# Narrower 120-row pieces, uneven over the rows, in a grouped 1x1 convolution

## The chip, the core and the metric

The kernel runs on one core of one Trainium2 chip. The metric is device time in microseconds (us). Most executions of one kernel lie within 0.5 us of each other; about one in five is longer (by 0.7 to 2.1 us). Ratios are computed as the mean time of one kernel's fast runs over that of the other's fast runs in the same rounds on the same chip, so they are not quite the ratios of the medians that are quoted.

## The reference

```
# x: (1, 512, 512, 192) bf16, w: (1, 1, 4, 48, 48) bf16
xg  = x.reshape(1, 512, 512, 4, 48)
out = einsum('bhwgc,gcd->bhwgd', xg, w[0, 0]).reshape(1, 512, 512, 192)
```

Every pixel (192 values, 384 bytes) is read once, multiplied by four 48x48 matrices and written once: 100.7 MB in and 100.7 MB out.

## The kernel before

Pixels are dealt to 128 rows (partitions). A "column" is one pixel on each row. SyncE issues the loads into a ring of three slots of 80 columns, TensorE transposes four columns at a time, VectorE copies the transposes out of PSUM, TensorE multiplies, ScalarE casts the product into an output ring and issues the stores.

What matters here is the plan of the transfers. Nearly all of them are `FULL`: 128 rows. Twice in the run, after 6 and after 11 further slots, a slot of 80 columns is filled in two parts: a **120-row piece** that leaves out rows 16 to 19 and 48 to 51, and a full piece for the rest of the slot. The blocks of a 120-row piece are listed as (queue, first row, rows, outer size, columns fewer):

```python
FULL = (("sync", 0, 128, 128, 0),)

PARTIAL = (
    ("sync", 0, 16, 4, 0), ("sync", 32, 16, 4, 0),
    ("pool", 52, 44, 11, 0), ("pool", 20, 12, 3, 0), ("pool", 96, 32, 8, 0),
)
UNEVEN = (("sync", 0, 16, 4, 16), *PARTIAL[1:])
FRONT = ((6, ((48, PARTIAL), (32, FULL))), (11, ((48, UNEVEN), (32, FULL))))

FILL_ROWS = 5
FILL_BEFORE = (2, 3)

# plan_fields: what the gaps leave out comes back as more columns at the end
    cols = npix - sum((n - b[4]) * b[2] for n, blocks in parts for b in blocks)

# transfers: the DRAM side of a block is seen as (outer, rows / outer, pixels)
            px = ap[pix:pix + rows * cols, :]
            ...
                view = px.rearrange("(c a i) n -> a c (i n)", a=outer, c=rows // outer)
            yield n, view, tile[r0:r0 + rows, at * C:(at + (c1 - c0 if f.full else cols)) * C]

# GpSimd: a tiny filler transfer of 5 rows ahead of some of its blocks
                    for n, dram, sbuf in transfers(xf, ring, p, ("pool",)):
                        if n in FILL_BEFORE:
                            filler()
                        gp.dma_start(sbuf, dram).then_inc(ld_sem[ld_key[p.i, n]], 16)
```

The rows in the gap keep stale values; their products are computed and never stored.

Of the kernel before, what the change touches and what calls it, by code (L numbers as in the profile page):

```python
# [38 lines left out]
FULL = (("sync", 0, 128, 128, 0),)  # L39

PARTIAL = (
    ("sync", 0, 16, 4, 0), ("sync", 32, 16, 4, 0),
    ("pool", 52, 44, 11, 0), ("pool", 20, 12, 3, 0), ("pool", 96, 32, 8, 0),
)
UNEVEN = (("sync", 0, 16, 4, 16), *PARTIAL[1:])
FRONT = ((6, ((48, PARTIAL), (32, FULL))), (11, ((48, UNEVEN), (32, FULL))))

FILL_ROWS = 5
FILL_BEFORE = (2, 3)


class Field:
# [31 lines left out]
def plan_fields(npix):  # L84

    parts, head = [], sum(HEAD)
    for slots, special in FRONT:
        parts += [(head + BIG * slots, FULL), *special]
# [91 lines left out]
def bass_standalone__grouped__vision_kernel(nc, x, w, out):  # L180
# [23 lines left out]
    def transfers(ap, tile, part, queues):  # L204
        f, c0, c1, at = part.field, part.c0, part.c1, part.at
        for n, (queue, r0, rows, outer, pix, cols) in enumerate(f.blocks):
            if queue not in queues:
                continue
            px = ap[pix:pix + rows * cols, :]
            if f.full:  # L210
                view = px.rearrange("(p i) n -> p (i n)", p=rows)[:, c0 * C:c1 * C]
            else:
                assert (c0, c1) == (0, f.cols)
                view = px.rearrange("(c a i) n -> a c (i n)", a=outer, c=rows // outer)
            yield n, view, tile[r0:r0 + rows, at * C:(at + (c1 - c0 if f.full else cols)) * C]
# [12 lines left out]
    with ExitStack() as es:  # L228
# [36 lines left out]
        def freed(p):  # L265

            return max(0, -(-(4 * p.g1 - RCOLS) // 8))

        @block.gpsimd
        def _(gp):  # L270
            gp.memset(esel[:], 1.0).then_inc(p0_sem, 1)  # L271
            gp.memset(ident[:], 1.0).then_inc(p1_sem, 1)  # L272
            gp.wait_ge(p0_sem, 1)
            gp.affine_select(out=esel[:], in_=esel[:], pattern=[[-1, ECOLS]],  # L274
                             compare_op=AluOpType.is_equal, fill=0.0, base=ESHIFT,
                             channel_multiplier=1).then_inc(e_sem, 1)
            gp.wait_ge(p1_sem, 1)
            gp.affine_select(out=ident[:], in_=ident[:], pattern=[[-1, 128]],  # L278
                             compare_op=AluOpType.is_equal, fill=0.0, base=0,
                             channel_multiplier=1).then_inc(id_sem, 1)  # L280
            used = []

            def filler():
                k = len(used)
                src = xf[0:2 * FILL_ROWS, 0:4].rearrange("(t p) n -> p t n", t=2)
                dst = fill[:, 8 * k:8 * k + 8].rearrange("p (t n) -> p t n", t=2)
                gp.dma_start(dst, src).then_inc(fill_sem[k], 16)  # L287
                used.append(k)

            for nth, u in enumerate(mixed):  # L290
                part = [p for p in u.pieces if not p.full]
                for p in part:
                    gp.wait_ge(t_done, freed(p))
                    for n, dram, sbuf in transfers(xf, ring, p, ("pool",)):
                        if n in FILL_BEFORE:
                            filler()
                        gp.dma_start(sbuf, dram).then_inc(ld_sem[ld_key[p.i, n]], 16)  # L297
                for p in u.pieces:
                    for n in range(len(p.blocks)):
                        gp.wait_ge(ld_sem[ld_key[p.i, n]], 16)  # L300
                gp.sem_inc(ld_sem[unit_keys[u][0]], 16)  # L301
                gp.wait_ge(go_sem, nth + 1)
                for i, s in enumerate(stores):
                    if any(s.field is p.field for p in part):
                        for n, dram, sbuf in transfers(of, oring, s, ("pool",)):
                            if n in FILL_BEFORE:
                                filler()
                            gp.dma_start(dram, sbuf).then_inc(st_sem[i][n], 16)  # L308
            for k in used:
                gp.wait_ge(fill_sem[k], 16)  # L310
# [174 lines left out]
```

## Time and profile before

| | before |
|---|---|
| median of the runs | 476.39 us |
| span of the profiled run | 474.6 us |
| bytes moved, mean rate | 201.54 MB, 425 GB/s |
| TensorE / ScalarE / VectorE busy | 90% / 82% / 52% |
| DMA busy (three queues, 16 engines) | 99.3% |

How to read it: the busy shares of the compute engines are high, but none is full, while all sixteen DMA engines are full from the second slice to the last but one. The prediction below shows these lines. What a page does not give is which of the sixteen engines is busy with what; that was worked out from the packet records of the trace, as the prediction describes.

### The profile page before, as it was taken

The numbers are of one execution on the slowest core, as the hardware profiler recorded it, in microseconds if no ns is written. First come the engines' busy times: TensorE is split into PE (matmuls) and PEld (weight loads), VectorE is DVE, ScalarE is ACT, GpSimd is POOL, SyncE is SP. The second block draws the span as 40 slices with busy tenths as digits, with TensorE's granted clock in tenths as the row PEclk, the third lists the DMA queues.
The fourth block names the chain that finished last, engine by engine and source line by source line (L and its number), as shares of the span: only waits on it lengthen the run. The fifth ranks groups of instructions, "written<-read, shape, count | busy, mean of one in ns | idle before, by whom it ended". The sixth has DMA issues, their size and how long they took to land.

```text
span 474.6 us, 13600 instructions
## 1 busy us (share of the span) xinstructions
PE 428.2 (90%) x6178; PEld 386.2 (81%) x6178; DVE 246.8 (52%) x258; ACT 388.4 (82%) x515; POOL 12.5 (3%) x28
## 2 busy tenths in 40 slices
PE   5999999999598999999999997989698997999990
PEld 4888898888487888888888986888597896988880
DVE  2655555555344555565555554545445553555550
ACT  2999998888567998889899986888678995998982
POOL 1000000200002000000000000100002000000000
PEclk9999999999889999999999999999979998999997
DMA  8999999999999999999999999999999999999997
GB/s 330 437 396 429 432 425 432 423 429 436 433 439 426 424 436 424 436 441 429 433 429 437 420 433 431 439 417 437 432 437 418 435 433 423 437 423 436 434 419 325
DMA packets 10528, 201.54 MB, mean 425 GB/s; under 512 B 2096, under 2 KB 2096, under 8 KB 2736
## 3 DMA queue, kind: packets, MB, share of 16 engines
q1 hardware_dynamic: 4320, 97.44, 48.1%
q10 hardware_dynamic: 4976, 97.42, 47.9%
q0 software_dynamic: 1216, 6.49, 3.3%
q8 instruction: 7, 0.11, 0.1%
q14 instruction: 9, 0.07, 0.0%
HBM read 100.68 MB, written 100.66 MB: 424 GB/s over the span
## 4 chain that ended last, share of the span: by engine, by line
PE 63%; DMA 20%; ACT 10%; another core or an unknown queue 2%; issue 1%; ACTq 1%; SPq 0%; POOLq 0%
PE o_ps L371 37%; PE xT_ps L351 27%; DMA out_dram<-oring 11%; ACT oring L450 10%; DMA ring<-in_x_dram 10%; ACTq L431 1%; SPq L321 0%; SPq L314 0%; ACTq L424 0%; POOLq L301 0%; POOLq L300 0%; ACTq L433 0%
## 5 line engine op out<-in xcount | busy, mean ns | idle before, releaser
L450 ACT CAST oring<-o_ps 128x768 bf16<-128x768 f32 x514 | 387.1, 801 | 76.6 <-PE o_ps L371 55.1
L413 DVE COPY xT_sb<-xT_ps 128x1536 bf16<-128x1536 bf16 x257 | 246.2, 958 | 212.4 <-PE xT_ps L351 212.4
L371 PE MATMUL o_ps<-wt,xT_sb 128*128 128x144 bf16 (+1 forms) x3084 | 288.4, 236 | 23.7 <-ACT oring L450 18.4
L371 PEld LDWEIGHTS o_ps<-wt,xT_sb 128*128 128x128 bf16 x3084 | 211.3, 99 | 62.2 <-ACT oring L450 52.4
L351 PE MATMUL xT_ps<-ident,ring 128*128 128x128 bf16 x3084 | 220.4, 222 | 9.9 <-POOLq L301 6.0
L351 PEld LDWEIGHTS xT_ps<-ident,ring 128*128 128x128 bf16 x3084 | 188.1, 99 | 13.2 <-POOLq L301 6.2
L287 POOL DMA_DIRECT2D fill<-in_x_dram x8 | 4.6, 573 | 349.4 <-PE xT_ps L351 227.0
L297 POOL DMA_DIRECT2D ring<-in_x_dram x6 | 3.3, 559 | 0.0
L308 POOL DMA_DIRECT2D out_dram<-oring x6 | 3.3, 555 | 0.0
L333 PE MATMUL o_ps<-w_sb,esel 48*128 48x48 bf16 x10 | 0.6, 211 | 2.8 <-DMA w_sb<-in_w_dram 2.8
L333 PEld LDWEIGHTS o_ps<-w_sb,esel 48*128 48x128 bf16 x10 | 0.5, 111 | 2.8 <-issue 2.8
L406 DVE CAST wt<-o_ps 128x480 bf16<-128x480 f32 x1 | 0.7, 657 | 3.4 <-PE o_ps L333 3.4
L450 ACT ACT_TABLE_LOAD x1 | 1.3, 1283 | 0.8 <-PEq L470 0.8
L274 POOL TENSOR_SCALAR_AFFINE_SELECT esel<-esel 48x272 bf16<-48x272 bf16 x1 | 0.4, 402 | 0.0
L271 POOL MEMSET esel<- 48x272 bf16 x1 | 0.3, 318 | 0.3 <-POOLq L470 0.3
L278 POOL TENSOR_SCALAR_AFFINE_SELECT ident<-ident 128x128 bf16<-128x128 bf16 x1 | 0.3, 282 | 0.0
L272 POOL MEMSET ident<- 128x128 bf16 x1 | 0.2, 198 | 0.0
L470 POOL MEMSET const-float32-0.0<- 128x1 f32 x1 | 0.1, 98 | 0.3 <-issue 0.3
L470 POOL MEMSET const-bfloat16-1.0<- 128x1 bf16 x1 | 0.1, 101 | 0.0
L470 POOL MEMSET const-uint8-127<- 128x1 uint8 x1 | 0.1, 101 | 0.0
L470 POOL MEMSET const-float32-1.0<- 128x1 f32 x1 | 0.1, 98 | 0.0
## 6 DMA issues: line engine op xcount, KB each, us to landing
ring<-in_x_dram SPq DMA_DIRECT2D x22, 3840.0 KB, 28.3
out_dram<-oring ACTq DMA_DIRECT2D x16, 3456.0 KB, 41.0
out_dram<-oring ACTq DMA_DIRECT2D x5, 3648.0 KB, 38.2
out_dram<-oring ACTq DMA_DIRECT2D x3, 1536.0 KB, 33.4
out_dram<-oring ACTq DMA_DIRECT2D x2, 2112.0 KB, 19.8
ring<-in_x_dram SPq DMA_DIRECT2D x2, 1536.0 KB, 38.1
out_dram<-oring ACTq DMA_DIRECT2D x1, 3072.0 KB, 36.5
out_dram<-oring ACTq DMA_DIRECT2D x1, 2688.0 KB, 51.0
```

What stands on the lines that cost most here:

```text
L274: gp.affine_select(out=esel[:], in_=esel[:], pattern=[[-1, ECOLS]], compare_op=AluOpType.is_equal, fill=0.0, base=ESHIFT, channel_multipli ...
L287: gp.dma_start(dst, src).then_inc(fill_sem[k], 16)
L297: gp.dma_start(sbuf, dram).then_inc(ld_sem[ld_key[p.i, n]], 16)
L308: gp.dma_start(dram, sbuf).then_inc(st_sem[i][n], 16)
L333: last = pe.matmul(o_ps[:, NOB - 1, col:col + CG], lhsT=esel[:, s0:s0 + 128], rhs=w_sb[:, g, :], start=True, stop=True, skip_group_check=True)
L351: last = pe.transpose(xT_ps[:, g % NXP, j * 128:(j + 1) * 128], xg[:, j * 128:(j + 1) * 128], ident[:])
L371: last = pe.matmul(o_ps[:, v % NOB, c0_:c1_], lhsT=xs[:, j * 128:(j + 1) * 128], rhs=wt[:, WOFF[tc]:WOFF[tc] + (c1_ - c0_)], start=(tc == ...
L406: dve.tensor_copy(wt[:], o_ps[:, NOB - 1, 0:WCOLS]).then_inc(wc_sem, 1)
L413: dve.tensor_copy(xT_sb[pair % NXS][:, 0:n * 2 * UC].rearrange("p (g c) -> p g c", g=n), xT_ps[:, b0:b0 + n, 0:2 * UC]).then_inc(e_done[pa ...
L431: act.dma_start(dram, sbuf).then_inc(st_sem[i][n], 16)
L450: act.copy(out_columns(g).rearrange("p (u c) -> p u c", u=2), o_ps[:, v % NOB:v % NOB + 2, 0:UC]).then_inc(fa_done[g % (2 * NTOK)] if g < ...
L470: nc = _bacc.Bacc("TRN2", target_bir_lowering=False, num_devices=1)
```

## The change

The change makes both 120-row pieces narrower (48 to 40 columns, the full pieces behind them grow from 32 to 40), so that the DMA engine that moves rows 16 to 19 and 48 to 51, called engine 4 here (the names are told with the prediction), is relieved less. In the second piece it shortens rows 96 to 127 by 4 columns and cuts the block of rows 0 to 15 into four quarters with different widths. As blocks are now numbered differently, the fillers are tied to the first row of a block instead of its number.

```diff
-UNEVEN = (("sync", 0, 16, 4, 16), *PARTIAL[1:])
-FRONT = ((6, ((48, PARTIAL), (32, FULL))), (11, ((48, UNEVEN), (32, FULL))))
+UNEVEN = (
+    ("sync", 0, 4, 1, 12), ("sync", 4, 4, 1, 16), ("sync", 8, 4, 1, 20), ("sync", 12, 4, 1, 16),
+    *PARTIAL[1:4], ("pool", 96, 32, 8, 4),
+)
+FRONT = ((6, ((40, PARTIAL), (40, FULL))), (11, ((40, UNEVEN), (40, FULL))))
 
 FILL_ROWS = 5
-FILL_BEFORE = (2, 3)
+FILL_BEFORE = (52, 20)
...
-                        if n in FILL_BEFORE:
+                        if p.field.blocks[n][1] in FILL_BEFORE:
```

More of the change, by code (lines that the diff above doesn't have):

```diff
@@ L305, in _ @@
                         for n, dram, sbuf in transfers(of, oring, s, ("pool",)):
-                            if n in FILL_BEFORE:
+                            if s.field.blocks[n][1] in FILL_BEFORE:
                                 filler()
```

## The prediction

The packet records carry no engine number, so the engine numbers in this document are names for groups of rows. The groups can be read from the traces. Linked by their gaps alone (a packet starts 3 to 4 ns before the end of the one before it), the records of the changed kernel from 303 to 337 us, where its second 120-row piece is loaded, form sixteen chains; one early link is ambiguous:

- Four carry one packet of each quarter (10,752, 9,216, 7,680 and 9,216 bytes) and four of the block of rows 32 to 47 (15,360 bytes): "engines 0 to 3", or "of rows 0 to 15".
- One carries no packet of the piece, so that its eight rows are the eight left out. It holds 30 of the 32 lengthened packets, with 1.36 us of lengthening in all: the slow engine, "engine 4".
- Three carry eight packets of the two blocks of rows 20 to 31 and 52 to 95: "engines 5 to 7".
- Eight carry four packets of these blocks and four of rows 96 to 127: "engines 8 to 15", or "of rows 64 to 127".

Each of the sixteen carries eight packets of the full piece that follows. Which number is which inside a group, and which of rows 52 to 95 are whose, is not shown. In the kernel before, four chains have four packets of each of the two 16-row blocks (12,288 and 18,432 bytes, from 306 to 322 us), eleven have packets of the GpSimd blocks, and one, the lengthened one, has none of the piece.

The even split of a quarter over four engines (the 96 pixels per engine below) was an estimate: the trace showed it for 16-row blocks, not for blocks of 4 rows. That the store queue hides the three stores more rests on this: the store issued at 342.8 us took 52.2 us to land, so stores were waiting around 345 us.

> **What bounds the kernel now.** I read the slice table first, then the queues, the groups, the waits, the last of the timeline, and last the single DMA packet records of the trace.
>
> ```profile
> PE   5999999999598999999999997989698997999990
> DMA  8999999999999999999999999999999999999997
> GB/s 330 437 396 429 432 425 432 423 429 436 433 439 426 424 436 424 436 441 429 433 429 437 420 433 431 439 417 437 432 437 418 435 433 423 437 423 436 434 419 325
> ...
> q1 hardware_dynamic: 4320, 97.44, 48.1%
> q10 hardware_dynamic: 4976, 97.42, 47.9%
> q0 software_dynamic: 1216, 6.49, 3.3%
> ```
>
> The DMA row is full in every slice but the first and the last. The three queues add up to 48.1 + 47.9 + 3.3 = 99.3% of sixteen engines' span (q1 loads, q10 stores, q0 what GpSimd issues). No compute engine is so full:
>
> ```profile
> PE 428.2 (90%) x6178; PEld 386.2 (81%) x6178; DVE 246.8 (52%) x258; ACT 388.4 (82%) x515; POOL 12.5 (3%) x28
> ...
> L450 ACT CAST oring<-o_ps 128x768 bf16<-128x768 f32 x514 | 387.1, 801 | 76.6 <-PE o_ps L371 55.1
> L371 PE MATMUL o_ps<-wt,xT_sb 128*128 128x144 bf16 (+1 forms) x3084 | 288.4, 236 | 23.7 <-ACT oring L450 18.4
> L351 PE MATMUL xT_ps<-ident,ring 128*128 128x128 bf16 x3084 | 220.4, 222 | 9.9 <-POOLq L301 6.0
> ```
>
> PE's only long wait is 6.0 us for the first mixed piece, and the DMA row stays at 9 through it. The chain of waits gives PE 63%[...]; I do not take that for the bound. The timeline of the end settles it:
>
> ```profile
> 464.62 0.34 ACTq L431 DMA_DIRECT2D out_dram<-oring  x1
> 465.00 0.80 ACT L450 CAST oring<-o_ps 128x768 bf16<-128x768 f32 x1 [0.21 <-issue]
> 465.83 0.34 ACTq L431 DMA_DIRECT2D out_dram<-oring  x1
> ```
>
> The last store is issued at 466.2 us of a 474.6 us span, so the final 8 us are a backlog of stores. The kernel ends when the last of sixteen DMA engines has emptied its queue. The question is only **which engine is last, and by how much**.
>
> The packet records have a start, a duration, a size and a queue, but no engine number. A 30,720-byte packet takes 1,138 ns (27.0 bytes per ns) nearly every time, and the next packet on the same engine starts 3 to 4 ns before the end of its predecessor. So I chained records by these gaps and by each engine's known list of packets. Two things came out. (1) Counting open packets, from 20 us to 465 us there is no stretch of 150 ns in which fewer than sixteen are open: no engine ever starves. (2) One chain holds nearly every lengthened packet (the 27,648-byte packets take 1,030 to 1,150 ns there, 1,025 elsewhere), about 19.5 us of excess in all, some 5% of its work. That chain holds none of the packets of the 120-row pieces. This is the slow engine, and **relieving it is what the 120-row pieces are for**.
>
> The finish of each chain before the end of the run: the slow engine 5.8 us; the four chains that fit the list of the engines of rows 0 to 15: 3.9, 3.2, 0.3 and 0.2 us; the others from 2.9 to 0.0 us. The very last one fits rows 64 to 127 and rows 20 to 31 about equally well.
>
> [...]
>
> **The change part by part.** All in pixels per engine; a pixel is 384 bytes in and 384 out, 768 / 27.0 = 28.4 ns of its engine.
>
> *Compute:* nothing. Columns in all stay 2,056: the missing pixels were 8 x 48 + 8 x 48 + 16 x 16 = 1,024, and are now 8 x 40 + 8 x 40 + 4 x (12 + 16 + 20 + 16) + 32 x 4 = 1,024. The instruction lists show the same 514 evictions, and the same PE work.
>
> *Engine 4:* its gap shrinks from 96 to 80 columns of 8 rows: +128 pixels, 98 KB, 128 x 28.4 ns = +3.64 us; with 5% of slowness +3.8. Its finish moves from 5.8 us before the end to about 2.0 us before it. It was early, so this costs nothing.
>
> *Engines 8 to 15:* 4 columns on 4 rows each: -16 pixels, -0.45 us.
>
> *Engines 5 to 7:* unchanged. Their latest is about 0.9 us before the end (or 0.0, if the last chain is one of them).
>
> *Engines 0 to 3:* the second piece's load of 16 rows x 32 columns becomes four of 4 rows x 28, 24, 20 and 24 columns. [...] 28 + 24 + 20 + 24 = 96 pixels per engine, where there were 4 x 32 = 128. The first piece gives 4 x 8 = 32 fewer as well, and the two full pieces behind them, 32 columns and now 40, give 32 more each: the total of each engine is **unchanged**. Two of these engines end 0.2 and 0.3 us before the end.
>
> *Issues:* three more loads and three more stores. An issue on ACT took 0.34 us, so ACT loses 1.0 us around 345 us; it is 82% busy, and the store queue is never empty, so this is hidden.
>
> *Sum:* if the last engine is one of 8 to 15, it moves 0.45 us earlier, and the next, an engine of rows 0 to 15 at 0.2 us, sets the end: -0.2 us. If it is one of 5 to 7: 0.0. I take -0.1: 476.39 - 0.1 = **476.3 us**.
>
> **The rivals.**
>
> *The slow engine becomes the last.* It would have to gain over 5.8 us; it gains 3.8. Against this too: its late position in the middle. Its loads land +2.8 us behind those of a normal engine at their worst (near 295 us), and the first relief shrinks by 1.8 us, so +4.6 us. Loads take 28.3 us from issue to landing, and PE never waited for a plain load over 1.6 us, so at most a short PE stall. If the whole 3.8 us counted: 480.
>
> *The quarter transfers fall on one engine* [...]. Engine 0 would then carry 4 x 96 = 384 pixels instead of 96: +288, +8.2 us, an end at up to 484.5. [...]
>
> *Each quarter goes to its own engine,* as 12, 16, 20, 16 suggests was meant: +16, 0, -16, 0 pixels, so 0.45 us either way on two of the four engines. Depending on which two are late: 475.9 to 476.6.
>
> *A gain beyond this* has no place: all finishes at their mean would be about 2 us earlier (474.4), and the change moves under 0.5 us off any engine that is late.
>
> **Range and chances.** Runs before spread by 0.4 us (476.16 to 476.57). The named effects reach from -0.5 to about +1.5 us; I give the range 475.5 to 477.6. Over 2% either way is 9.5 us: faster is out of reach by the sum above (0.01); slower needs the one-engine rival and something more (0.02); within 2%: 0.97.
>
> **What would show it.** Right: the same PE, ACT and DVE busy times; the DMA row full up to the last slice; slow engine's chain ending about 2 us before the end instead of 5.8; q1 and q10 packet counts up only by the few packets of the split. Wrong: one chain of engines 0 to 3 ending several us after the others (one-engine rival); the slow chain last; PE waiting longer than 6.0 us for a mixed piece, or a slice of the DMA row below 9 in the middle (the lag rival).

## The result, and the profile after

The changed kernel took 476.32 us (median of 6, 476.22 to 478.40), the kernel before 476.39 us in the same rounds. The ratio is 1.0007, with a 95% interval of 0.9987 to 1.0028: the same. A second measurement on another chip, below, gave 0.9991 (0.9977 to 1.0005).

The page of the changed kernel, slices, queues and compute (the slice rows are tenths of busy time in 40 equal slices; the queue rows are packets, MB and the share of sixteen engines' span):

```profile
PE 430.8 (91%) x6178; PEld 389.0 (82%) x6178; DVE 246.9 (52%) x258; ACT 388.7 (82%) x515; POOL 12.5 (3%) x28
...
DMA  8999999999999999999999999999999999999997
...
DMA packets 10552, 201.54 MB, mean 425 GB/s; under 512 B 2120, under 2 KB 2120, under 8 KB 2768
...
q1 hardware_dynamic: 4332, 98.03, 48.4%
q10 hardware_dynamic: 4988, 98.01, 48.2%
q0 software_dynamic: 1216, 5.31, 2.7%
```

The instruction counts are those of before (6,178 matmuls, 515 on ACT), the DMA row is the same, and the share of the three queues is again 99.3%. The narrower pieces show only in how the bytes are dealt: q0, which carries the GpSimd blocks, fell from 6.49 to 5.31 MB, and q1 and q10 took that over.

The packet counts hold a finer fact. q1 and q10 grew by 12 packets each, all of 4 bytes (492 on q1 where there were 480, 572 on q10 where there were 560). In the trace of the kernel before, the block of 16 rows is four data packets and then one of 4 bytes on each of four chains, 16 + 4 = 20 in all. Four quarters of 4 rows are 4 x (4 + 4) = 32 if each is split over four engines with a 4-byte packet on each, and 4 x (4 + 1) = 20 if each runs on one. The measured +12 says: **each quarter is split one row to each of four engines**. The chains show the same: each of the four has one packet of every quarter, with a 4-byte packet behind it.

The last store is issued later than before, and still well ahead of the end (timeline of ACT, start and duration in us; 465.83 us before):

```profile
467.57 0.80 ACT L453 CAST oring<-o_ps 128x768 bf16<-128x768 f32 x1 [0.20 <-issue]
468.40 0.34 ACTq L434 DMA_DIRECT2D out_dram<-oring  x1
```

The backlog of stores behind it shrinks from 8.4 to 5.9 us, at the same end. This point moves from run to run: other kernels with the same time issue their last store at 465.0 to 467.9 us. It does not set the end as long as a backlog is left.

From the packet records of the changed kernel: from the slow engine's finish to the end it is now about 2.7 us (2.4 in a second trace), where it was 5.8. The engines of rows 0 to 15 again fall into two groups. Two end early (both 3.2 us before the end), two late: 1.0 and 0.0 us. Both late chains carry packets of the instruction queue q14 ("instruction packets" below), 5 of them in one and 4 in the other; the early ones carry none. Each such packet takes 309 ns, and most of the packets that follow one on its engine are lengthened by 240 to 620 ns. (The records were chained a second time, with the list of packets that each engine has to move as a constraint. The finishes given here came out the same, and the finishes given below from packet records are of this second chaining.)

### The profile page after: what moved, and what is told of

Read it like the earlier page. It is cut to its first block, busy times and chain, and to the rows that moved or that the text cites. A ratio compares the mean times of both kernels' runs of the same rounds, so it can differ in the third digit from the quotient of the medians.

```text
span 474.6 us, 13609 instructions
## 1 busy us (share of the span) xinstructions
PE 430.8 (91%) x6178; PEld 389.0 (82%) x6178; DVE 246.9 (52%) x258; ACT 388.7 (82%) x515; POOL 12.5 (3%) x28
## 3 DMA queue, kind: packets, MB, share of 16 engines
q0 software_dynamic: 1216, 5.31, 2.7%
## 4 chain that ended last, share of the span: by engine, by line
PE 63%; DMA 20%; ACT 10%; another core or an unknown queue 2%; ACTq 2%; issue 1%; SPq 0%; POOLq 0%
PE o_ps L374 37%; PE xT_ps L354 26%; DMA out_dram<-oring 10%; ACT oring L453 10%; DMA ring<-in_x_dram 9%; ACTq L434 2%; SPq L324 0%; SPq L317 0%; ACTq L427 0%; POOLq L304 0%; POOLq L303 0%; ACTq L436 0%
```

## The experiments

The theory: in both kernels no DMA engine runs out of work before the last stores (from 20 to 465 us fewer than sixteen packets are open for 35 ns in all in the kernel before, and never in the changed one), so the run ends with the engine that has the most work for its speed. Engine 4 (rows 16 to 19 and 48 to 51) is some 4% slower: 19.5 us of lengthening in about 445 us of work (15,680 pixels x 28.4 ns). Before the change it had slack (time between its finish and the end of the run), and the change uses some of it up. The only other load that the change moves is 0.45 us off each of engines 8 to 15, which is worth at most the 0.2 us to the next engine. The rivals: the gaps do nothing and the bytes in all (or the compute chain) set the time; engine 4 was last already; the quarters move work between engines 0 to 3.

Every experiment is an edit of the changed kernel, moves the same bytes in all and computes the right result.

### No gap at all

```diff
-FRONT = ((6, ((40, PARTIAL), (40, FULL))), (11, ((40, UNEVEN), (40, FULL))))
+FRONT = ()
```

> The 120-row pieces are taken out: every transfer has 128 rows, so all sixteen DMA engines carry the same 16,384 pixels. Theory (the last DMA engine ends the run, and engine 4 is the slow one): against the changed kernel engine 4 carries 576 pixels more, 576 x 28.4 ns x 1.05 = 17.2 us; it ended 3.4 us before the end in the changed kernel's trace, so the run grows by about 13.8 us, to 490 us. Rival (the total of bytes, or the compute chain, sets the time, and the uneven pieces do nothing): 476.3 as before, within 1 us, since the bytes are the same.

Measured: 489.64 us (489.12 to 489.92), ratio to the kernel before 1.0273. The rival of the bytes falls. Its page shows an end that neither of the two kernels has (slice rows), and a window view of the last stretch shows how many engines are left (columns: window, its length, busy time and count for PE, PEld, DVE, ACT and POOL, granted clock, DMA share, GB/s):

```profile
DMA  8999999999999999999999999999999999999961
GB/s 330 437 388 422 444 424 433 428 434 436 429 430 430 433 440 426 425 430 439 440 423 433 437 433 430 422 439 437 429 427 428 440 423 431 431 434 424 399 269 53
```

```profile
474.00:482.00 8.00, 0.00 (x0) 0.00 (x0) 0.00 (x0) 0.00 (x0) 0.00 (x0) 0.64 0.31 120
482.00:488.00 6.00, 0.00 (x0) 0.00 (x0) 0.00 (x0) 0.00 (x0) 0.00 (x0) 0.50 0.05 20
```

No compute engine works after 474 us. In the last window the run has 487.3 - 482 = 5.3 us left, and the DMA share of 0.05 x 16 engines x 6 us is 4.8 us of engine time: **one** engine is running, and 20 GB/s x 6 us / 5.3 us = 23 GB/s is near the 27 bytes per ns of one engine's largest packets. In the packet records fifteen chains end within 0.2 us of each other, and the sixteenth 11.2 us after them. The kernel waits for a single slow engine. This kernel also issues no transfer from GpSimd at all, so that queue isn't what makes the engine slow.

### The gap on other rows

```diff
-    ("sync", 0, 16, 4, 0), ("sync", 32, 16, 4, 0),
-    ("pool", 52, 44, 11, 0), ("pool", 20, 12, 3, 0), ("pool", 96, 32, 8, 0),
+    ("sync", 0, 20, 5, 0), ("sync", 32, 20, 5, 0),
+    ("pool", 56, 40, 10, 0), ("pool", 24, 8, 2, 0), ("pool", 96, 32, 8, 0),
...
-    ("sync", 0, 4, 1, 12), ("sync", 4, 4, 1, 16), ("sync", 8, 4, 1, 20), ("sync", 12, 4, 1, 16),
-    *PARTIAL[1:4], ("pool", 96, 32, 8, 4),
+    ("sync", 0, 20, 5, 16),
+    *PARTIAL[1:4], ("pool", 96, 32, 8, 2),
...
-FILL_ROWS = 5
-FILL_BEFORE = (52, 20)
+FILL_ROWS = 6
+FILL_BEFORE = (56, 24)
```

> The gap of eight rows is moved from engine 4 (rows 16 to 19 and 48 to 51) to engine 5 (rows 20 to 23 and 52 to 55); the pieces stay 40 columns wide and 1,024 pixels are missing in all, as now. Theory: engine 4 is back at the mean load, +576 pixels = +17.2 us, ending about 13.8 us later than now: 490 us, as without any gap[...]. Rival (any row gap of this size does the same, for instance by giving the queues slack): 476.3.

Measured: 490.00 us (489.88 to 490.33), ratio 1.0281. A gap of the same size four rows further on is worth nothing (the name "engine 5" takes for granted that rows 20 to 23 and 52 to 55 share an engine, which no trace shows); the end looks as it does without a gap:

```profile
DMA  8999999999999999999999999999999999999861
```

Again one chain ends last and alone, 9.4 us after the other fifteen, and it carries the list of rows 0 to 19. It is engine 4 that has to be relieved. Why it is slow, no run here shows. Both runs are of one chip; but in the traces from the two other chips (one block, for example, and the changed kernel measured again) the slow chain is also the one without a packet of the 120-row pieces.

### Narrower still: 32 and 24 columns

```diff
-FRONT = ((6, ((40, PARTIAL), (40, FULL))), (11, ((40, UNEVEN), (40, FULL))))
+FRONT = ((6, ((32, PARTIAL), (48, FULL))), (11, ((32, UNEVEN), (48, FULL))))   # or 24 and 56
-    *PARTIAL[1:4], ("pool", 96, 32, 8, 4),
+    *PARTIAL[1:4], ("pool", 96, 32, 8, 8),                                        # or 12
```

> The 120-row pieces shrink further, from 40 to 32 columns, and rows 96 to 127 are 8 instead of 4 shorter in the second, so that the total stays. Engine 4 gets 128 more pixels: +3.8 us. Theory: it ended 3.4 us before the end, so it now is the last by about 0.4 us: 476.3 to 477.0. If the change of this study had already used up the slack (rival: engine 4 was last already), the run would grow by the whole 3.8 us: 480.1. If the relief does nothing: 476.3.

> The pieces shrink to 24 columns, rows 96 to 127 are 12 shorter in the second. Engine 4 gets 256 pixels more than in the changed kernel: +7.6 us. Theory (slack of 3.4 us, then slope one): +4.2 us, 480.5. Rival without slack: +7.6 us, 483.9. Rival where the relief does nothing: 476.3.

Measured: 477.48 us (477.28 to 479.06, ratio 1.0022) at 32 columns and 481.12 us (480.76 to 483.13, ratio 1.0090) at 24. Against 476.32 us at 40 columns that is +1.2 and +4.8 us. From 32 to 24 columns the step is 3.6 us, close to the 3.8 us that 128 pixels more cost on engine 4; from 40 to 32 it is only 1.2, and from 48 to 40, the change, it is 0. So the changed kernel sits 3.8 - 1.2 = 2.6 us before the knee, the point at which the slack is used up. The first step was 0.5 us above its expected range: the 3.4 us of slack written there was a first reading of the chain, which loses its identity in the last 4 us; the later reading of 2.7 us fits both runs (3.8 - 2.7 = 1.1 and 7.6 - 2.7 = 4.9). The same slack puts the run without a gap at 17.2 - 2.7 = 14.5 us over the changed kernel; 13.3 were measured. A smaller slowness alone does not explain the difference: 576 pixels at the plain 28.4 ns already make 16.4 us, 13.7 after the slack. What else the run without a gap saves is not shown.

The profiled executions of both runs are long ones (478.57 and 483.13 us), so their pages are not pages of the medians. In both, a chain of rows 0 to 15 ends last, and the slow engine 1.3 and 2.3 us before it, at 475.5 and 479.1 us. The spans of the other executions begin at just these figures, 475.5 and 479.0 us. So if engine 4 ends at the same time in the ordinary executions, which were not profiled, it is last there, as the theory says. What makes the long ones long seems to lie elsewhere: at 24 columns the packets on the four engines of rows 0 to 15 take 32 us more in all than is usual for their sizes, and 24 us in the long execution profiled under "Work moved" below, against 8 us in the changed kernel. Why, no run shows.

At 24 columns the lag of engine 4 also shows on the other side of the kernel. The waits of PE for the mixed pieces (us in total, times, longest), in the changed kernel and at 24 columns:

```profile
PE xT_ps L354 <- POOLq L304: 6.6, 2, 5.4
```

```profile
PE xT_ps L354 <- POOLq L304: 17.7, 2, 10.5
```

The profiled run at 24 columns issues its last store at 474.9 us, and before that its DMA engines are short of stores (the same window in the changed kernel, then at 24 columns):

```profile
458.00:466.00 8.00, 6.79 (x99) 5.87 (x97) 4.10 (x5) 6.69 (x10) 0.00 (x0) 1.00 1.00 426
458.00:466.00 8.00, 7.70 (x114) 6.84 (x113) 4.49 (x5) 6.98 (x11) 0.00 (x0) 1.00 0.79 336
```

So past the knee two things grow together: engine 4's own backlog, and the delay of the compute engines that wait for engine 4's rows. Engine 4's own finish moved by 7.2 us (471.9 to 479.1 us), no more than the 7.6 us of its 256 pixels, so its backlog alone would account for the end of the ordinary executions. What the delay adds, and how much of it belongs to the long execution, is not shown.

### One block instead of four quarters

```diff
-    ("sync", 0, 4, 1, 12), ("sync", 4, 4, 1, 16), ("sync", 8, 4, 1, 20), ("sync", 12, 4, 1, 16),
+    ("sync", 0, 16, 4, 16),
```

> Only the four quarters are undone: rows 0 to 15 of the second piece go as one block, 16 columns shorter, as in the kernel before; the rest is the changed kernel. Theory (each quarter of 4 rows is itself split one row to each of engines 0 to 3, so the 12, 16, 20, 16 are shared evenly and three issues more on two queues are hidden): no difference to the changed kernel, 476.3 within 0.3 us. Rival (each quarter runs on one engine of its own): two engines differ by 16 pixels, 0.45 us, and the time by up to that, either way.

Measured: 476.28 us (475.98 to 476.62), ratio 0.9995 (0.9982 to 1.0009). No difference to the kernel before, nor to 476.3 of the changed one. q1 has 4,320 packets here, 12 fewer than with the quarters, as counted above:

```profile
q1 hardware_dynamic: 4320, 98.03, 48.4%
q10 hardware_dynamic: 4976, 98.01, 48.2%
```

### Quarters far apart

```diff
-    ("sync", 0, 4, 1, 12), ("sync", 4, 4, 1, 16), ("sync", 8, 4, 1, 20), ("sync", 12, 4, 1, 16),
+    ("sync", 0, 4, 1, 0), ("sync", 4, 4, 1, 0), ("sync", 8, 4, 1, 32), ("sync", 12, 4, 1, 32),
```

> The four quarters of rows 0 to 15 become 0, 0, 32 and 32 columns shorter, where the changed kernel has 12, 16, 20 and 16; the sum is 64 as now. Theory (every quarter is split one row to each of engines 0 to 3): each engine's load is unchanged, 476.3 within 0.4 us. Rival (quarter n runs on engine n alone): engines 0 and 1 get 48 to 64 pixels more (+1.4 to +1.8 us) and engines 2 and 3 as many fewer. The pair run put a late engine among 0 and 1, since it cost 1.9 us, so this would give 477.7 to 478.1.

Measured: 476.09 us (475.99 to 476.35), ratio 0.9985 (0.9972 to 0.9999). With the widths of the quarters as far apart as this, nothing gets longer, where the rival asked for 1.4 us or more. The 0.2 us below the changed kernel on the same chip is not something that one measurement settles.

### No relief for rows 0 to 15

```diff
-    ("sync", 0, 4, 1, 12), ("sync", 4, 4, 1, 16), ("sync", 8, 4, 1, 20), ("sync", 12, 4, 1, 16),
-    *PARTIAL[1:4], ("pool", 96, 32, 8, 4),
+    ("sync", 0, 16, 4, 0),
+    *PARTIAL[1:4], ("pool", 96, 32, 8, 12),
```

> Rows 0 to 15 of the second piece keep all 40 columns; rows 96 to 127 are 12 instead of 4 shorter, so that the total stays. Engines 0 to 3 get 64 pixels more each (+1.8 us), engines 8 to 15 get 32 fewer (-0.9 us). Theory (the last engine of the changed kernel is one of engines 0 to 3, the one with instruction packets in its queue): +1.8 us, 478.1. Rival (the last one is one of engines 8 to 15): no growth, 475.9 to 476.8.

Measured: 477.99 us (477.75 to 478.25), ratio 1.0034; against the kernel before (476.24 us on this chip) +1.75 us, where 1.8 was expected. The 64 pixels come out one for one in the time. So an engine of rows 0 to 15 is last. This also shows what the shortening of those rows, which both kernels have, is for. In its packet records the chains with 4 and with 5 instruction packets end 0.0 and 0.5 us before the end, and the engines of rows 64 to 127 2.2 to 5.0 us before it.

### Work moved from engines 2 and 3 to 0 and 1

```diff
-    ("sync", 0, 4, 1, 12), ("sync", 4, 4, 1, 16), ("sync", 8, 4, 1, 20), ("sync", 12, 4, 1, 16),
-    *PARTIAL[1:4], ("pool", 96, 32, 8, 4),
+    ("sync", 0, 12, 4, 16), ("sync", 12, 4, 2, 16),
+    ("sync", 32, 12, 4, 0), ("sync", 44, 4, 2, 0), *PARTIAL[2:4], ("pool", 96, 32, 8, 4),
```

> In the second piece the blocks of rows 0 to 15 and 32 to 47 are cut into 12 rows over engines 0 to 3 and 4 rows over engines 0 and 1, so 64 pixels (1.8 us) go from each of engines 2 and 3 to each of engines 0 and 1. In both traces two of these four engines carry 4 and 5 instruction packets and end about 3 us later than the other two. If those two are 2 and 3: the run ends with another engine, 0.5 to 0.9 us earlier (475.5 to 475.8). If one or both are 0 or 1: +1.8 us, 478.1. Rival (which of these engines carries what does not matter): 476.3.

Measured: 478.21 us (477.98 to 480.87), ratio 1.0038; +1.97 us over the kernel before on this chip. q1 has 4,324 packets here and 4,320 with one block. That is the +4 of two blocks of 12 rows with 12 + 4 packets and two of 4 rows with 4 + 2, where two of 16 rows have 16 + 4: the 4-row blocks run on two engines each, called 0 and 1. That both use the same two is not in the counts, but the cost of 1.97 us agrees with the 1.8 us of 64 pixels on one engine. At least one of the two late engines is 0 or 1: the chain with five instruction packets that ends this run fits only the longer list. Where the other one is stays open; the profiled run was one of the long executions (480.87 us), and its chains with four such packets could not be told apart.

### Both kernels' successor, tried

```diff
-    ("sync", 0, 4, 1, 12), ("sync", 4, 4, 1, 16), ("sync", 8, 4, 1, 20), ("sync", 12, 4, 1, 16),
-    *PARTIAL[1:4], ("pool", 96, 32, 8, 4),
+    ("sync", 0, 16, 4, 24),
+    *PARTIAL[1:4], ("pool", 96, 32, 8, 2),
...
-FRONT = ((6, ((40, PARTIAL), (40, FULL))), (11, ((40, UNEVEN), (40, FULL))))
+FRONT = ((6, ((36, PARTIAL), (44, FULL))), (11, ((36, UNEVEN), (44, FULL))))
```

> An attempt at a kernel that beats both: the 120-row pieces are 36 columns wide, rows 0 to 15 of the second are 24 shorter in one block, rows 96 to 127 are 2 shorter; 1,024 pixels are missing as before. Against the changed kernel engines 0 to 3 get 32 pixels fewer (-0.9 us), engine 4 gets 64 more (+1.9 us), engines 8 to 15 get 8 more (+0.2 us). In the changed kernel's trace the last finish is on engines 0 to 3, one of engines 8 to 15 follows 0.7 us earlier and engine 4 about 3 us earlier. Theory: the end moves by 0.5 us to 475.8, the limit being then an engine of 8 to 15. Rival (engine 4's lag in the middle already costs): 476.3 or more.

> The changed kernel unaltered, beside the two others on one chip, as their base line. 476.3 within 0.3 us, ratio to the kernel before 1.000 within its interval.

Measured on one chip: the changed kernel again 476.30 us (476.20 to 476.61), ratio 0.9991; the attempt 476.23 us (475.54 to 478.17), ratio 0.9993 (0.9973 to 1.0014). Three of its six executions lie at 475.5 to 475.9 us, below every one of the changed kernel's, the other three at 476.55 and above. That is inconclusive: the gain expected was 0.5 us, and the interval is wider than that. In the profiled execution (476.55 us) the two engines of rows 0 to 15 with instruction packets still end last.

## Why the prediction was right

**The bound.** The prediction named the last DMA engine, against the 63% of the chain that lay on PE. The run without a gap shows it most plainly: in its last 5.3 us one DMA engine works and nothing else does.

**Engine 4's slack.** The step predicted +3.8 us on an engine that ended 5.8 us early, so no cost. The cost was none, and the engine now ends 2.7 us early (2.0 predicted), so the step took 3.2 us of its slack (3.5 by the second trace) and not 3.8. Two readings of the prediction were a little off: 19.5 us of excess are 4.4% of the engine's work, not 5%, and of the "others" the earliest ended 2.4 us before the end in the second chaining, where the prediction has 2.9. Neither moves the forecast. The size fits the runs around it: 128 pixels cost 0, 1.2 and 3.6 us, in this order, as the slack is used up.

**Engines 0 to 3.** The prediction counted each of the four quarters as shared by all four engines, so that they change nothing. That was an estimate then; the 12 packets more on each of two queues show it, and so do the two runs with the quarters undone and with them far apart.

**Who is last.** Here the prediction was undecided: it put the very last engine among those of rows 64 to 127 or 20 to 31, with two of rows 0 to 15 only 0.2 and 0.3 us behind. In the changed kernel an engine of rows 0 to 15 is last (64 pixels there cost 1.75 us). For the forecast it made little odds, as the prediction had sums for both cases: -0.1 us was predicted, -0.07 us is the difference of the medians, and the two ratios, 1.0007 and 0.9991, lie on both sides of one. A difference of this size is not resolved, nor was it claimed.

**Issues.** Three loads and three stores more were called hidden; the run with one block, which has none of them, takes the same time.

**The rival of the lag.** PE waited 6.6 us for the mixed pieces in two waits of at most 5.4 us, where it had one of 6.0 us; the DMA row stays full, and the longest wait is below the 6.0 us that the prediction had named as a sign of being wrong. The waits grow to 8.8 us at 32 columns and 17.7 us at 24, both in long executions; that they lengthen the run is not shown even there.

## What to carry to other kernels

When all DMA engines are full, ask which one ends last and how early the others are; giving work to an engine that ends early cost nothing here until its slack was gone: the first 128 pixels on an engine that ended 5.8 us early cost 0, the next 1.2 us and the third 3.6 us. A change that rebalances by less than the slack, and touches no engine that is last, can be forecast as "no change"; here that held within the 0.3% that the intervals resolve. To move work between engines, check in the packet counts where a transfer really runs: four transfers with four widths looked like four engines here, and the 12 packets more on each queue showed that they were not.
